# Loading K of pair 30 ahead of V of pair 29, with the usual split of pair 31's scores and a 24 KB + 8 KB last V

## The chip, the cores and the metric

The kernel runs on one core of one Trainium2 chip. The metric is device time in microseconds (us), the median of several executions. A profiled execution shows a span that is about 1.3 us shorter than its time (662.3 for a time of 663.57).

## The reference, cut to what matters

```python
B, D, Hq, Sk, Dh, F = 2, 512, 32, 8192, 128, 1376           # one query row per batch
q = layernorm(x) @ wq                                        # [B, 32 heads, 128]
scores = einsum("bhqd,bhkd->bhqk", q, k_cache) * Dh ** -0.5  # 64 (batch, head), 8192 keys each
o = einsum("bhqk,bhkd->bhqd", softmax(scores), v_cache)
h = x + o @ wo
h2 = h + ffn(layernorm(h))                                   # gate (ReLU), up, down
```

K and V together are 268 MB; each byte is used once. Everything else is small.

## The kernel before: the parts that matter

The kernel goes through 32 *pairs* (two heads of one batch). A K or a V of a pair is one 4 MB load into one of four slots: slot 0 K of even pairs, slot 1 V of even pairs, slots 2 and 3 the same for odd pairs. All loads go through one queue in program order. `J = 128` blocks of keys make up a pair.

The scores of a pair are split. VectorE does 96 of the 128 blocks (one multiply of K by q, four adds that halve the width, one reduce). TensorE does the other 32 in `NG = 4` groups of 8 (transpose on TensorE, evacuation by ScalarE, product with q). ScalarE takes the exp of both parts, and TensorE multiplies by V ("PV"), 32 matmuls a pair. After two pairs TensorE collects their outputs and VectorE normalizes and spreads them.

Pairs 0 to 29 run in loops on each engine; pairs 30 and 31 are written out as a tail, with the output product (O x Wo, then Wp) and the FFN behind them. Pair 31 gets a split of its own, eight TensorE groups and 64 blocks for VectorE:

```python
def split(p):
    n = 2 * NG if p == NP - 1 else NG
    return n, J - n * GT
```

TensorE in the tail (cut):

```python
collect(tail, 1)                              # pairs 28 and 29
k_part(tail, P0, (2, 3, 4, 5), ((k2p, 1),))   # K30; waits for VectorE's release k2p
...                                           # o_gather, O x Wo (30 matmuls), Wp (8 matmuls)
k_part(tail, P1, (9, 10, 11, 12, 14, 15, 16, 17), ((k2p, 2),))  # K31: eight groups
pv(tail, P0, ...)
pv(tail, P1, ...)                             # z_sum between its two parts
```

VectorE in the tail. It first needs TensorE's collect, and it is VectorE that tells TensorE (`k2p`) that a K is in:

```python
if p >= P0:
    if p == P0:
        dve.wait(t_ob_loop)                   # collect of pairs 28 and 29
        normalize(Ob, dve.run, dve.last)
        o_spread(g - 1, dve, dve.run(o_scale()))
    nc.vector.wait_ge(g2d, p - P0 + 1)
    nc.vector.wait_ge(slot_sem[s], 16)        # K of pair p has landed
    nc.vector.sem_inc(k2p, 1)                 # releases TensorE's k_part
    dve.last()
    t_dm[p] = dve.run(k_mult(p))
    k_adds(p, dve.run, dve.last)
    t_s[p] = dve.run(k_reduce(p))
```

The end of the load order is K29, V29, K30, K31, V30, V31 (two rows of 16 KB a partition), W_up, W_gate, W_down. The weights go into slot 0, so after K30 has been read.

The softmax here doesn't subtract the row's maximum and nothing guards it: scores larger than these inputs give would overflow.

Of the kernel before, what the change touches and what calls it, by code (L numbers as in the profile page):

```python
# [9 lines left out]
ALU = mybir.AluOpType  # L10
# [29 lines left out]
def bass_sequential_preLN__gqa_block_cached__glu_gated_reglu__decode_kernel(  # L40
# [24 lines left out]
    FR = F - 10 * 128  # L65
    VJ = 4
    PG = 2
    DR = (H - 2) * Dh // 128
# [6 lines left out]
    with ExitStack() as es:  # L75
# [87 lines left out]
        if True:  # L163

            def program():
# [145 lines left out]

                def split(p):
                    n = 2 * NG if p == NP - 1 else NG
                    return n, J - n * GT

                EV = 13
# [12 lines left out]
                def k_part(T, p, ev, k_wait):  # L329
                    s, ng = (2 * p) % 4, split(p)[0]  # L330
                    k_t = tile(s)
# [3 lines left out]
                    def score(g):  # L335
                        wait(a2p, ev[g])
                        kv_ = kT[g % 2][:].rearrange("p (k n r) -> p k r n", n=128, r=2)
                        for k in range(GT // 2):
                            jj = g * GT + 2 * k
                            for r in range(2):  # L340
                                i = nc.tensor.matmul(  # L341
                                    Sp[p % 2][:, 2 * jj:2 * jj + 4], lhsT=kv_[:, k, r, :],
                                    rhs=q_c[p % 2][:, 4 * r:4 * r + 4], start=(r == 0), stop=(r == 1))
                                if loop and g == ng - 2 and k == r == 0:
                                    T.mark(("kf", p), i)
                        if not loop:
                            T.mark(("sc", p, g), i)
                        elif g == ng - 1:
                            i.then_inc(p2a, 1)

                    for w in k_wait:
                        wait(*w)
                    for g in range(ng):
                        if g >= 2:
                            wait(a2p, ev[g - 2])
                        for k in range(GT // 2):
                            j = split(p)[1] + g * GT + 2 * k
                            i = nc.tensor.transpose(  # L358
                                Tp[g % 2][:, k * 128:(k + 1) * 128],
                                k_t[:, j:j + 2, :].rearrange("p j d -> p (j d)").bitcast(F32), ident_f[:])  # L360
# [4 lines left out]
                        if g >= 1:  # L365
                            score(g - 1)
                    score(ng - 1)

# [44 lines left out]
                with nc.Fori(0, NI, engines=OrderedEngineSet([nc.tensor.engine])):  # L413
                    jd = split(0)[1]
                    k_part(body, 0, (1, 2, 3, 4), ((k2p, 1),))
                    collect(body, 6)
                    pv(body, 0, ((jd, J, ((slot_sem[1], 16), (a2p, 5))), (0, jd, ((a2p, 7),))))
                    k_part(body, 1, (8, 9, 10, 11), ((k2p, 2),))
                    nc.tensor.wait_ge(l2p, 1)
                    o_gather(body)  # L420
                    nc.tensor.sem_inc(l2p, -1)
                    pv(body, 1, ((jd, J, ((slot_sem[3], 16), (a2p, 12))), (0, jd, ((a2p, EV),))))
                    z_sum(Ob)
# [8 lines left out]
                P0, P1 = NP - 2, NP - 1  # L432
                j30, j31 = split(P0)[1], split(P1)[1]
                collect(tail, 1)
# [10 lines left out]
                tail.mark("op", i)  # L445
                nc.tensor.wait_ge(a2p, 8)
                for c in range(DC):
                    nc.tensor.matmul(  # L448
                        Wp[:, c * B:(c + 1) * B], lhsT=os_sb[:].rearrange("p (n c) -> p c n", c=DC)[:, c, :], rhs=sel2[:],
                        start=False, stop=False, skip_group_check=True)  # L450
                k_part(tail, P1, (9, 10, 11, 12, 14, 15, 16, 17), ((k2p, 2),))
                pv(tail, P0, ((j30, J, ((slot_sem[1], 16), (a2p, 6))), (0, j30, ((a2p, 13),))))
                pv(tail, P1, ((j31, J, ((sem_vl[0], 16), (a2p, 18))), (0, j31, ((a2p, 19), (sem_vl[1], 16)))),
                   lambda: tail.mark("z", z_sum(Sp[0])))
# [14 lines left out]
                def exp(p, k, src):  # L469
                    q, jd_ = p % PG, split(p)[1]  # L470
                    j0, j1 = ((jd_, J), (0, jd_))[k]
                    for a in range(2):
# [45 lines left out]
                def k_mult(p):  # L518
                    jd_ = split(p)[1]
                    return nc.vector.tensor_tensor(  # L520
                        out=prod[:, 0:jd_, :], in0=tile((2 * p) % 4)[:, 0:jd_, :],
                        in1=q_c[p % 2][:, 8:QW].unsqueeze(1).broadcast_to([128, jd_, Dh]), op=ALU.mult)

                def k_adds(p, run, last):
                    jd_, w = split(p)[1], Dh
                    while w > 8:
                        w //= 2
                        last()
                        run(nc.vector.tensor_tensor(  # L529
                            out=prod[:, 0:jd_, 0:w], in0=prod[:, 0:jd_, 0:w], in1=prod[:, 0:jd_, w:2 * w], op=ALU.add))  # L530
                    last()

                def k_reduce(p):
                    jd_ = split(p)[1]
                    return nc.vector.tensor_reduce(  # L535
                        out=scores[p % PG][:, 0:jd_], in_=prod[:, 0:jd_, 0:8], axis=AX.X, op=ALU.add)

                def exp_pe(p):
                    n_ = split(p)[0] * GT
                    exp(p, 0, lambda h, a: Sp[p % 2][h, 0:2 * n_].rearrange(  # L540
                        "p (g j a) -> p g j a", a=2, j=VJ)[:, :, :, a])

                def exp_dve(p):
                    exp(p, 1, lambda h, a: scores[p % PG][h, 0:split(p)[1]].rearrange("p (g j) -> p g j", j=VJ))

# [62 lines left out]
                for p in range(NP):  # L608
                    s = (2 * p) % 4
                    ng, jd = split(p)  # L610
                    g = p // 2

                    if p >= P0:
                        if p == P0:
                            dve.wait(t_ob_loop)
                            normalize(Ob, dve.run, dve.last)
                            o_spread(g - 1, dve, dve.run(o_scale()))
                        nc.vector.wait_ge(g2d, p - P0 + 1)
# [3 lines left out]
                        t_dm[p] = dve.run(k_mult(p))  # L622
                        k_adds(p, dve.run, dve.last)
                        t_s[p] = dve.run(k_reduce(p))

                    if p < P1:
# [6 lines left out]

                    def evacs(g0=0, g1=ng):
                        for gg in range(g0, g1):
                            act.wait(tokp("pt", p, gg))
                            if gg >= 2:
                                act.wait(tokp("sc", p, gg - 2))
                            elif p == P1:
                                act.wait(tokp("sc", p - 1, NG - 2 + gg))  # L640
                            evac(gg)

                    if p == P0:
                        act.wait(tokp("pv", p - 1))
                        sums()
                        evacs()
                        act.wait(tokp("sc", p, ng - 1))
                        exp_pe(p)
                        act.wait(tok("og", NI))
                        to_pe(nc.scalar.activation(  # L650
                            out=O_all[:].rearrange("p r b -> p b r"),
                            in_=Op[1][:, 0:B * DR].rearrange("p (b r) -> p b r", r=DR), func=ACT.Copy))
                        act.wait(tok("op", NI))
                        to_pe(nc.scalar.activation(out=os_sb[:], in_=Op[1][:], func=ACT.Copy))
                    elif p == P1:
                        evacs(0, NG)
                        act.wait(t_s[P0])
                        exp_dve(P0)
                        evacs(NG)
                        act.wait(tokp("sc", p, ng - 1))  # L660
                        exp_pe(p)
                        act.wait(t_s[P1])
                        exp_dve(P1)

                    if p + 2 < NP:
                        sp.wait((d2s, p + 1), tokp("kf", p))
                        load(s, A_k_cache, p + 2)
                    if p < NP - 4:
                        sp.wait(tokp("pv", p))
                        load((2 * p + 1) % 4, A_v_cache, p + 2)  # L670
                    elif p == NP - 3:
                        sp.wait(tokp("pv", NP - 4))
                        load(1, A_v_cache, NP - 2)
                        sp.wait(tokp("pv", NP - 3))
                        for k, (j0, j1) in enumerate(((J // 2, J), (0, J // 2))):
                            nc.sync.dma_start(
                                slot[3][:, j0 * Dh:j1 * Dh],
                                kv(A_v_cache, NP - 1)[:, j0 * Dh:j1 * Dh]).then_inc(sem_vl[k], 16)
                    elif p == NP - 2:
                        sp.wait(t_dm[p], tokp("pt", p, NG - 1))  # L680
# [14 lines left out]
                sums()  # L695
                collect(tail, 20)
                dve.wait(tok("ob", NI))
# [140 lines left out]
```

## Time and profile before

| | kernel before |
|---|---|
| time, median of 3 | 662.72 us (662.57 to 663.37) |
| moved | 281.19 MB at a mean of 425 GB/s |
| PV of the last pair ends | 651.33 |
| TensorE's first FFN product starts | 654.62 |
| VectorE's last instruction starts | 660.00 |

The page of the kernel before, part 4, follows the chain of waits back from the end. Its line by engine:

```profile
DMA 76%; DVE 16%; PE 5%; ACT 2%; issue 1%; SPq 0%; DVEq 0%; ACTq 0%
...
```

Three quarters of that chain is loads that follow on one another, and the page's DMA row is at 90% or more in 39 of its 40 slices. So what a change can win without moving fewer bytes is to be looked for in the tail. The tail's VectorE, from the timeline of the kernel before (start in us, duration in us, engine, line, operation, out<-in, count, and in brackets what ended an idle time):

```profile
611.84 0.95 DVE L535 TENSOR_REDUCE scores<-prod 128x96 f32<-128x768 bf16 x1
619.03 0.17 DVE L482 TENSOR_REDUCE zr<-Ob 128x4 f32<-128x8 f32 x1 [6.25 <-PE Ob L394]
...
620.14 6.55 DVE L520 TENSOR_TENSOR prod<-slot,q_c 128x12288 bf16<-128x12288 bf16 x1
626.73 6.74 DVE L529 TENSOR_TENSOR prod<-prod 128x6144 bf16<-128x6144 bf16 x4
633.50 0.95 DVE L535 TENSOR_REDUCE scores<-prod 128x96 f32<-128x768 bf16 x1
634.49 4.42 DVE L520 TENSOR_TENSOR prod<-slot,q_c 128x8192 bf16<-128x8192 bf16 x1
...
643.72 0.69 DVE L535 TENSOR_REDUCE scores<-prod 128x64 f32<-128x512 bf16 x1
```

VectorE stands idle for 6.25 us after pair 29 (612.8 to 619.0), because it waits for TensorE's collect before it may touch K30. From there it works without a pause to 644.4.

The same stretch on TensorE, from the timeline of the kernel before:

```profile
613.69 2.74 PE L382 MATMUL O<-slot,e 128*16 128x512 bf16 x24 [4.67 <-ACT e L474]
...
617.13 1.87 PE L394 MATMUL Ob<-sel,os_sb 128*128 128x4 f32 x8 [0.17 <-ACT os_sb L550]
619.95 1.97 PE L358 MATMUL T<-ident_f,slot 128*128 128x128 f32 x8 [0.95 <-DVEq L620]
...
631.61 2.03 PE L448 MATMUL W<-sel,os_sb 128*128 128x2 f32 x8 [0.69 <-ACT os_sb L654]
633.62 1.97 PE L358 MATMUL T<-ident_f,slot 128*128 128x128 f32 x8
...
645.16 4.88 PE L382 MATMUL O<-slot,e 128*16 128x512 bf16 x48
...
650.29 1.04 PE L382 MATMUL O<-slot,e 128*16 128x512 bf16 x16
```

L382 is PV, L394 collect, L358 the transposes of a K, L448 Wp.

Stretches of time of the kernel before (start:end, length; busy time of PE, PEld, DVE, ACT, POOL with counts; granted TensorE clock, which is the share of its full speed that TensorE was allowed; DMA share; GB/s). The clock records hold only 0.50 ("half clock") and 1.00 ("full clock"); other values are means over a stretch.

```profile
620.00:625.00 5.00, 4.74 (x40) 3.82 (x40) 5.00 (x5) 3.27 (x4) 0.00 (x0) 0.50 1.04 446
635.00:640.00 5.00, 4.74 (x49) 3.70 (x48) 4.97 (x2) 4.34 (x8) 0.00 (x0) 0.50 1.01 429
645.00:650.00 5.00, 5.00 (x57) 1.75 (x55) 0.00 (x0) 1.57 (x8) 0.00 (x0) 0.55 1.00 420
650.00:655.00 5.00, 3.45 (x54) 2.44 (x51) 1.18 (x8) 0.60 (x1) 0.00 (x0) 1.00 0.92 369
655.00:656.00 1.00, 1.00 (x38) 1.00 (x35) 0.33 (x2) 0.00 (x0) 0.00 (x0) 1.00 0.30 115
656.00:657.00 1.00, 1.00 (x40) 0.92 (x38) 0.47 (x2) 0.00 (x0) 0.00 (x0) 0.65 0.02 6
```

The stream runs dry in the microsecond after 655, while the FFN is still running at 660.

### The profile page before, as it was taken

The numbers are of one execution on the slowest core, as the hardware profiler recorded it, in microseconds if no ns is written. First come the engines' busy times: TensorE is split into PE (matmuls) and PEld (weight loads), VectorE is DVE, ScalarE is ACT, GpSimd is POOL, SyncE is SP. The second block draws the span as 40 slices with busy tenths as digits, with TensorE's granted clock in tenths as the row PEclk, the third lists the DMA queues.
The fourth block names the chain that finished last, engine by engine and source line by source line (L and its number), as shares of the span: only waits on it lengthen the run. The fifth ranks groups of instructions, "written<-read, shape, count | busy, mean of one in ns | idle before, by whom it ended". The sixth has DMA issues, their size and how long they took to land.

```text
span 662.3 us, 7890 instructions
## 1 busy us (share of the span) xinstructions
PE 331.6 (50%) x3221; PEld 200.0 (30%) x3221; DVE 467.6 (71%) x285; ACT 215.9 (33%) x432; POOL 71.9 (11%) x121
## 2 busy tenths in 40 slices
PE   2652344445455453555645453554436455343787
PEld 2431322224232122333323232331214233121464
DVE  1775576788767678776767877676887767688691
ACT  0631332243343223334223333422334332232351
POOL 2002002020200202020020202002020200202000
PEclk9995565555756556755555567555675555557557
DMA  9999999999999999999999999999999999999995
GB/s 380 427 416 432 433 435 427 435 428 431 436 429 433 431 428 435 433 429 435 426 433 435 428 435 431 429 433 433 426 440 424 435 431 429 433 433 426 440 414 231
DMA packets 10782, 281.19 MB, mean 425 GB/s; under 512 B 1202, under 2 KB 1556, under 8 KB 1940
## 3 DMA queue, kind: packets, MB, share of 16 engines
q1 hardware_dynamic: 10760, 281.06, 98.9%
q8 instruction: 6, 0.10, 0.1%
q14 instruction: 4, 0.03, 0.0%
q10 hardware_dynamic: 12, 0.00, 0.0%
HBM read 281.05 MB, written 0.00 MB: 424 GB/s over the span
## 4 chain that ended last, share of the span: by engine, by line
DMA 76%; DVE 16%; PE 5%; ACT 2%; issue 1%; SPq 0%; DVEq 0%; ACTq 0%
DMA slot<-in_A_k_cache_dram 76%; DVE prod L520 15%; PE O L382 1%; PE T L358 1%; DVE prod L529 1%; ACT kT L547 1%; PE O L442 1%; PE Ob L394 0%; PE S L341 0%; PE W L448 0%; ACT e L474 0%; PE O L739 0%; PE S L739 0%; PE O L791 0%; ACT os_sb L550 0%
## 5 line engine op out<-in xcount | busy, mean ns | idle before, releaser
L520 DVE TENSOR_TENSOR prod<-slot,q_c 128x12288 bf16<-128x12288 bf16 (+1 forms) x32 | 207.7, 6492 | 144.9 <-DMA slot<-in_A_k_cache_dram 142.9
L382 PE MATMUL O<-slot,e 128*16 128x512 bf16 x1024 | 119.0, 619 | 214.7 <-ACT e L474 151.1
L529 DVE TENSOR_TENSOR prod<-prod 128x6144 bf16<-128x6144 bf16 (+4 forms) x128 | 210.3, 1643 | 7.8
L547 ACT ACTIVATE kT<-T 128x1024 bf16<-128x1024 bf16 x132 | 130.3, 1022 | 149.6 <-PE T L358 146.6
L358 PE MATMUL T<-ident_f,slot 128*128 128x128 f32 x528 | 117.6, 379 | 30.2 <-DVEq L568 29.1
L382 PEld LDWEIGHTS O<-slot,e 128*16 128x16 bf16 x1024 | 26.1, 113 | 281.8 <-ACT e L474 178.7
L358 PEld LDWEIGHTS T<-ident_f,slot 128*128 128x128 f32 x528 | 84.7, 194 | 45.6 <-DVEq L568 44.5
L474 ACT ACTIVATE e<-scores 64x96 bf16<-64x96 f32 (+1 forms) x64 | 19.4, 303 | 239.2 <-DVEq L582 238.8
L516 POOL COPY q_c<-q_all 128x136 bf16<-128x136 bf16 x32 | 57.1, 1788 | 198.2 <-DVEq L572 168.0
L341 PE MATMUL S<-q_c,kT 128*128 128x4 bf16 x1056 | 49.2, 169 | 39.2 <-ACT kT L547 38.5
L341 PEld LDWEIGHTS S<-q_c,kT 128*128 128x128 bf16 x1056 | 41.1, 105 | 68.0 <-ACT kT L547 66.6
L394 PE MATMUL Ob<-sel,os_sb 128*128 128x4 f32 x136 | 31.0, 351 | 24.0 <-ACT os_sb L550 24.0
L394 PEld LDWEIGHTS Ob<-sel,os_sb 128*128 128x128 f32 x136 | 29.5, 321 | 25.9 <-ACT os_sb L550 25.9
L499 POOL MEMSET O_l<- 128x40 bf16 (+1 forms) x13 | 1.8, 135 | 303.9 <-DVEq L579 303.9
L535 DVE TENSOR_REDUCE scores<-prod 128x96 f32<-128x768 bf16 (+1 forms) x32 | 30.2, 945 | 2.8
L547 ACT ACT_TABLE_LOAD x15 | 19.2, 1283 | 0.3
L474 ACT ACTIVATE e<-S 64x32 bf16<-64x32 f32 (+1 forms) x64 | 13.0, 203 | 15.2 <-PE S L341 14.8
L474 ACT ACTIVATION_READ_ACCUMULATOR e<-S 64x1 f32 x64 | 12.8, 201 | 0.7
L550 ACT ACTIVATE os_sb<-O 128x512 f32<-128x512 f32 x17 | 10.1, 597 | 7.7 <-PE O L382 7.3
L474 ACT ACTIVATION_READ_ACCUMULATOR e<-scores 64x1 f32 x64 | 11.8, 184 | 0.0
L403 PEld LDWEIGHTS Ob<-zs,ones_f 128*128 128x128 f32 x30 | 7.3, 303 | 12.7 <-issue 12.7
L299 ACT ACTIVATE q_all<-O 128x512 bf16<-128x512 f32 x8 | 4.4, 596 | 17.9 <-PE O L294 17.9
(94 smaller groups left out, 90.9 us busy)
## 6 DMA issues: line engine op xcount, KB each, us to landing
slot<-in_A_k_cache_dram SPq DMA_DIRECT2D x32, 4096.0 KB, 32.1
slot<-in_A_v_cache_dram SPq DMA_DIRECT2D x31, 4096.0 KB, 30.3
slot<-in_A_wq_dram SPq DMA_DIRECT2D x1, 4096.0 KB, 12.4
slot<-in_A_v_cache_dram SPq DMA_DIRECT2D x2, 2048.0 KB, 27.8
X<-in_A_wo_dram SPq DMA_DIRECT2D x1, 3840.0 KB, 46.7
slot<-in_B_W_up_dram SPq DMA_DIRECT2D x1, 1376.0 KB, 23.5
slot<-in_B_W_gate_dram SPq DMA_DIRECT2D x1, 1376.0 KB, 26.4
slot<-in_B_W_down_dram SPq DMA_DIRECT2D x2, 512.0 KB, 27.6
```

The source lines that it names most:

```text
L341: i = nc.tensor.matmul(Sp[p % 2][:, 2 * jj:2 * jj + 4], lhsT=kv_[:, k, r, :], rhs=q_c[p % 2][:, 4 * r:4 * r + 4], start=(r == 0), stop=(r ...
L358: i = nc.tensor.transpose(Tp[g % 2][:, k * 128:(k + 1) * 128], k_t[:, j:j + 2, :].rearrange("p j d -> p (j d)").bitcast(F32), ident_f[:])
L382: i = nc.tensor.matmul(Op[0][c:c + 16, :], lhsT=e_t[q][:, j // VJ, :], rhs=v_t[:, j:j + VJ, :].rearrange("p j d -> p (j d)"), start=(q == ...
L394: i = nc.tensor.matmul(Ob[:, 0:4], lhsT=os_sb[:, jj * Dh:(jj + 1) * Dh], rhs=sel[:, 4 * jj:4 * jj + 4], start=(jj == 0), stop=(jj == VJ - 1))
L403: return nc.tensor.matmul(bank[:, ZC:ZC + 8], lhsT=ones_f[:], rhs=zs[:], start=True, stop=True)
L474: i = nc.scalar.activation(out=e_t[q][h, j0 // VJ:j1 // VJ, 8 * q:8 * q + 8].rearrange("p g (j a) -> p g j a", a=2)[:, :, :, a], in_=src(h ...
L516: nc.gpsimd.tensor_copy(out=q_c[p % 2][:], in_=q_all[:, p]).then_inc(g2d, 1)
L520: return nc.vector.tensor_tensor(out=prod[:, 0:jd_, :], in0=tile((2 * p) % 4)[:, 0:jd_, :], in1=q_c[p % 2][:, 8:QW].unsqueeze(1).broadcast ...
L529: run(nc.vector.tensor_tensor(out=prod[:, 0:jd_, 0:w], in0=prod[:, 0:jd_, 0:w], in1=prod[:, 0:jd_, w:2 * w], op=ALU.add))
L535: return nc.vector.tensor_reduce(out=scores[p % PG][:, 0:jd_], in_=prod[:, 0:jd_, 0:8], axis=AX.X, op=ALU.add)
L547: to_pe(nc.scalar.activation(out=kT[gg % 2][:], in_=Tp[gg % 2][:].bitcast(BF16), func=ACT.Copy))
L550: to_pe(nc.scalar.activation(out=os_sb[:], in_=Op[0][:], func=ACT.Copy))
```

## The change

Intent: K30 is loaded ahead of V29, so that it is there when VectorE has finished pair 29. VectorE then does K30 at once and the normalize and spread of pairs 28 and 29 behind it. That leaves it the time for the usual 96 blocks of pair 31, and TensorE's eight groups for pair 31 become four. The last V comes as rows of 24 KB and 8 KB, so that only 8 PV matmuls hang on the last piece.

```diff
+    V_LAST = 32
...
-                def split(p):
-                    n = 2 * NG if p == NP - 1 else NG
-                    return n, J - n * GT
...
-                k_part(tail, P1, (9, 10, 11, 12, 14, 15, 16, 17), ((k2p, 2),))
-                pv(tail, P0, ((j30, J, ((slot_sem[1], 16), (a2p, 6))), (0, j30, ((a2p, 13),))))
-                pv(tail, P1, ((j31, J, ((sem_vl[0], 16), (a2p, 18))), (0, j31, ((a2p, 19), (sem_vl[1], 16)))),
+                k_part(tail, P1, (10, 11, 12, 13), ((k2p, 2),))
+                pv(tail, P0, ((JC, J, ((slot_sem[1], 16), (a2p, 6))), (0, JC, ((a2p, 8),))))
+                pv(tail, P1, ((V_LAST, J, ((sem_vl[0], 16), (a2p, 15))), (0, V_LAST, ((a2p, 15), (sem_vl[1], 16)))),
...
                     if p >= P0:
-                        if p == P0:
-                            dve.wait(t_ob_loop)
-                            normalize(Ob, dve.run, dve.last)
-                            o_spread(g - 1, dve, dve.run(o_scale()))
                         nc.vector.wait_ge(g2d, p - P0 + 1)
...
                         k_adds(p, dve.run, dve.last)
+                        if p == P0:
+                            dve.wait(tokp("pv", p - 2))
                         t_s[p] = dve.run(k_reduce(p))
+                        if p == P0:
+                            dve.wait(t_ob_loop)
+                            normalize(Ob, dve.run, dve.last)
+                            o_spread(g - 1, dve, dve.run(o_scale()))
...
-                    if p < NP - 4:
-                        sp.wait(tokp("pv", p))
-                        load((2 * p + 1) % 4, A_v_cache, p + 2)
-                    elif p == NP - 3:
...
-                        for k, (j0, j1) in enumerate(((J // 2, J), (0, J // 2))):
+                    v_loads = [p] if p < NP - 5 else [NP - 5] if p == NP - 4 else [NP - 4, NP - 3] if p == NP - 3 else []
+                    for r in v_loads:
+                        sp.wait(tokp("pv", r))
+                        if r < NP - 3:
+                            load((2 * r + 1) % 4, A_v_cache, r + 2)
+                    if p == NP - 3:
+                        for k, (j0, j1) in enumerate(((V_LAST, J), (0, V_LAST))):
```

(ScalarE does pair 30's second exp right after pair 30's own work and no longer in the middle of pair 31's; `split(p)` becomes a constant everywhere.)

More of the change, by code (lines that the diff above doesn't have):

```diff
@@ L329, in k_part @@
                 def k_part(T, p, ev, k_wait):
-                    s, ng = (2 * p) % 4, split(p)[0]
+                    s = (2 * p) % 4
                     k_t = tile(s)
@@ L343, in score @@
                                     rhs=q_c[p % 2][:, 4 * r:4 * r + 4], start=(r == 0), stop=(r == 1))
-                                if loop and g == ng - 2 and k == r == 0:
+                                if loop and g == NG - 2 and k == r == 0:
                                     T.mark(("kf", p), i)
@@ L347, in score @@
                             T.mark(("sc", p, g), i)
-                        elif g == ng - 1:
+                        elif g == NG - 1:
                             i.then_inc(p2a, 1)
@@ L352, in k_part @@
                         wait(*w)
-                    for g in range(ng):
+                    for g in range(NG):
                         if g >= 2:
@@ L356, in k_part @@
                         for k in range(GT // 2):
-                            j = split(p)[1] + g * GT + 2 * k
+                            j = JC + g * GT + 2 * k
                             i = nc.tensor.transpose(
@@ L366, in k_part @@
                             score(g - 1)
-                    score(ng - 1)
+                    score(NG - 1)
                 def pv(T, p, parts, between=None):
@@ L413, in program @@
                 with nc.Fori(0, NI, engines=OrderedEngineSet([nc.tensor.engine])):
-                    jd = split(0)[1]
                     k_part(body, 0, (1, 2, 3, 4), ((k2p, 1),))
                     collect(body, 6)
-                    pv(body, 0, ((jd, J, ((slot_sem[1], 16), (a2p, 5))), (0, jd, ((a2p, 7),))))
+                    pv(body, 0, ((JC, J, ((slot_sem[1], 16), (a2p, 5))), (0, JC, ((a2p, 7),))))
                     k_part(body, 1, (8, 9, 10, 11), ((k2p, 2),))
@@ L421, in program @@
                     nc.tensor.sem_inc(l2p, -1)
-                    pv(body, 1, ((jd, J, ((slot_sem[3], 16), (a2p, 12))), (0, jd, ((a2p, EV),))))
+                    pv(body, 1, ((JC, J, ((slot_sem[3], 16), (a2p, 12))), (0, JC, ((a2p, EV),))))
                     z_sum(Ob)
@@ L432, in program @@
                 P0, P1 = NP - 2, NP - 1
-                j30, j31 = split(P0)[1], split(P1)[1]
                 collect(tail, 1)
@@ L445, in program @@
                 tail.mark("op", i)
-                nc.tensor.wait_ge(a2p, 8)
+                nc.tensor.wait_ge(a2p, 9)
                 for c in range(DC):
@@ L469, in exp @@
                 def exp(p, k, src):
-                    q, jd_ = p % PG, split(p)[1]
-                    j0, j1 = ((jd_, J), (0, jd_))[k]
+                    q = p % PG
+                    j0, j1 = ((JC, J), (0, JC))[k]
                     for a in range(2):
@@ L518, in k_mult @@
                 def k_mult(p):
-                    jd_ = split(p)[1]
                     return nc.vector.tensor_tensor(
-                        out=prod[:, 0:jd_, :], in0=tile((2 * p) % 4)[:, 0:jd_, :],
-                        in1=q_c[p % 2][:, 8:QW].unsqueeze(1).broadcast_to([128, jd_, Dh]), op=ALU.mult)
+                        out=prod[:, 0:JC, :], in0=tile((2 * p) % 4)[:, 0:JC, :],
+                        in1=q_c[p % 2][:, 8:QW].unsqueeze(1).broadcast_to([128, JC, Dh]), op=ALU.mult)
                 def k_adds(p, run, last):
-                    jd_, w = split(p)[1], Dh
+                    w = Dh
                     while w > 8:
@@ L529, in k_adds @@
                         run(nc.vector.tensor_tensor(
-                            out=prod[:, 0:jd_, 0:w], in0=prod[:, 0:jd_, 0:w], in1=prod[:, 0:jd_, w:2 * w], op=ALU.add))
+                            out=prod[:, 0:JC, 0:w], in0=prod[:, 0:JC, 0:w], in1=prod[:, 0:JC, w:2 * w], op=ALU.add))
                     last()
                 def k_reduce(p):
-                    jd_ = split(p)[1]
                     return nc.vector.tensor_reduce(
-                        out=scores[p % PG][:, 0:jd_], in_=prod[:, 0:jd_, 0:8], axis=AX.X, op=ALU.add)
+                        out=scores[p % PG][:, 0:JC], in_=prod[:, 0:JC, 0:8], axis=AX.X, op=ALU.add)
                 def exp_pe(p):
-                    n_ = split(p)[0] * GT
+                    n_ = NG * GT
                     exp(p, 0, lambda h, a: Sp[p % 2][h, 0:2 * n_].rearrange(
@@ L543, in exp_dve @@
                 def exp_dve(p):
-                    exp(p, 1, lambda h, a: scores[p % PG][h, 0:split(p)[1]].rearrange("p (g j) -> p g j", j=VJ))
+                    exp(p, 1, lambda h, a: scores[p % PG][h, 0:JC].rearrange("p (g j) -> p g j", j=VJ))
                 def evac(gg):
@@ L609, in program @@
                     s = (2 * p) % 4
-                    ng, jd = split(p)
                     g = p // 2
                     if p >= P0:
-                        if p == P0:
-                            dve.wait(t_ob_loop)
-                            normalize(Ob, dve.run, dve.last)
-                            o_spread(g - 1, dve, dve.run(o_scale()))
                         nc.vector.wait_ge(g2d, p - P0 + 1)
@@ L632, in program, with evacs @@
                             q_copy(p + 1)
-                    def evacs(g0=0, g1=ng):
-                        for gg in range(g0, g1):
+                    def evacs():
+                        for gg in range(NG):
                             act.wait(tokp("pt", p, gg))
@@ L641, in evacs @@
                             evac(gg)
+                        act.wait(tokp("sc", p, NG - 1))
+                        exp_pe(p)
                     if p == P0:
@@ L646, in program @@
                         evacs()
-                        act.wait(tokp("sc", p, ng - 1))
-                        exp_pe(p)
                         act.wait(tok("og", NI))
@@ L652, in program @@
                             in_=Op[1][:, 0:B * DR].rearrange("p (b r) -> p b r", r=DR), func=ACT.Copy))
+                        act.wait(t_s[p])
+                        exp_dve(p)
                         act.wait(tok("op", NI))
@@ L655, in program @@
                     elif p == P1:
-                        evacs(0, NG)
-                        act.wait(t_s[P0])
-                        exp_dve(P0)
-                        evacs(NG)
-                        act.wait(tokp("sc", p, ng - 1))
-                        exp_pe(p)
-                        act.wait(t_s[P1])
-                        exp_dve(P1)
+                        evacs()
+                        act.wait(t_s[p])
+                        exp_dve(p)
                     if p + 2 < NP:
@@ L667, in program @@
                         load(s, A_k_cache, p + 2)
-                    if p < NP - 4:
-                        sp.wait(tokp("pv", p))
-                        load((2 * p + 1) % 4, A_v_cache, p + 2)
-                    elif p == NP - 3:
-                        sp.wait(tokp("pv", NP - 4))
-                        load(1, A_v_cache, NP - 2)
-                        sp.wait(tokp("pv", NP - 3))
-                        for k, (j0, j1) in enumerate(((J // 2, J), (0, J // 2))):
+                    v_loads = [p] if p < NP - 5 else [NP - 5] if p == NP - 4 else [NP - 4, NP - 3] if p == NP - 3 else []
[5 more added lines that the diff above has]
+                        for k, (j0, j1) in enumerate(((V_LAST, J), (0, V_LAST))):
                             nc.sync.dma_start(
@@ L678, in program @@
                                 kv(A_v_cache, NP - 1)[:, j0 * Dh:j1 * Dh]).then_inc(sem_vl[k], 16)
-                    elif p == NP - 2:
+                    if p == NP - 2:
                         sp.wait(t_dm[p], tokp("pt", p, NG - 1))
@@ L695, in program @@
                 sums()
-                collect(tail, 20)
+                collect(tail, 16)
                 dve.wait(tok("ob", NI))
```

## The prediction

> **What bounds it now.** The page gives 281.19 MB at a mean of 425 GB/s, DMA busy in tenths at 9 in 39 of 40 slices, and the chain of waits is 76% DMA. [...] One 4 MB load takes about 9.7 us. The change moves no byte, so nearly all of the 662.7 us stays. What can move is the tail after the stream. By windows of time the DMA share is 1.00 at 652-654 us, 0.66, 0.30 and 0.02 in the next microseconds: the last bytes arrive near 656.5. The kernel ends at 662.3. Behind the attention TensorE is the chain: pair 29's PV ends 616.4, collect to 619.0, K of 30 from 619.95, its scores to 626.1, O x Wo 627.35-630.9, Wp 631.6-633.6, K of 31 in eight groups 633.6-645.1, PV of 30 and 31 645.16-651.33, then 11 us of output and FFN.
>
> **What changes.** Stream today (landings): K29 598.2, V29 607.9, K30 617.7, K31 627.4, V30 637.1, V31 646.9, FFN weights up to 656.5. After: K29 598.2, K30 607.9, V29 617.7, the rest in place. The issues still come in time: K30 is issued at 585.6 (K28's multiply done), V29 right behind, K31 at 605, V30 at 605.4, V31 once pair 29's PV is done (about 621, while the queue has work to 637), weights near 629 (queue to 647). So I expect no DMA gap.
>
> - VectorE: K30's multiply starts at 612.9 (pair 29's reduce) instead of 620.1; with 6.56+6.74+0.95 us it ends at 627.2, then normalize and spread (1.1), K31's full multiply 628.4-642.7. VectorE ends a microsecond earlier than before (644.4) though it multiplies 96 columns of pair 31 instead of 64.
> - TensorE: V29 lands 9.7 later, so pair 29's PV ends near 621.0 (32 matmuls in 3.3 us after 617.7) instead of 616.4: +4.6. Collect is followed directly by K30 (today 0.95 us of wait for normalize): K30 from 623.5, i.e. +3.6. Pair 31 has four groups instead of eight: 6.2 us instead of 11.5, -5.3. PV of 30 begins at 643.4 instead of 645.16: -1.7.
> - PV of 30 and 31 is the same 64 matmuls (0.10 us each at granted clock 0.50, about 0.06 at 1.00). exp of pair 31 is out by 645.2, before PV of 30 is done. V31's 3 MB land near 644.4, its last 1 MB at 646.9: no wait. End of PV near 649.7; [...]
>
> **On the path.** About 1.6 us of tail. A floor is set by the weights: the last W_down block lands at 656.5 and the FFN's last product ends at 659.9, so no more than about 2.8 us can be won without waiting for the weights.
>
> **Prediction.** 661.2 us, 80% range 660.2 to 662.6. Faster by over 2%: 0.01; within 2%: 0.98; slower by over 2%: 0.01.
>
> **Signs.** Right: DMA still full to 655-656; K30 multiply near 612.9; PE waits for V29 until about 617.7; PV of pair 31 ends 648.5-650; FFN waits on no weight, or only briefly. Wrong steps would show as: a DMA gap near 605, 621 or 629; VectorE's score of 31 later than 643.5; PE waiting for V31's last piece; FFN groups waiting for DMA.
>
> **What would make it wrong.** V31's issue waiting past 637 (then each us of gap is a us lost); slower DMA with the 24 KB and 8 KB rows; TensorE at half clock in all of PV and FFN, which would eat the 1.6 us; or weights landing later.

The sum: 4.6 us later with V29, 3.6 at the start of K30, 5.3 us less for the four groups, so PV begins 1.7 us earlier and ends near 649.7 instead of 651.33. That is about 1.6 us, and 662.7 less that is about the 661.2. The remarks under "What would make it wrong" on a gap, on 24 KB and 8 KB rows and on half clock are estimates; only the rows were put to a test (runs 11 and 12). What single steps took at each clock can be read in the kernel before: collect 1.87 us at 0.50 (from 617.13) and 1.05 at 1.00 (from 652.03), 24 PV products 2.74 us at 0.50 (from 613.69), 16 of them 1.04 at 1.00 (from 650.29).

## More of the kernel before

K31 starts at 633.62, exactly when Wp ends (631.61 + 2.03 = 633.64) and also just when VectorE issues pair 30's reduce (633.50) and with it K31's release.

TensorE is 95% busy in 620 to 625 and 635 to 640 and still has the half clock, 0.50. These two stretches are mostly transposes.

## The result, and the profile after

| | before | after |
|---|---|---|
| time, median of 4 | 662.64 us (661.88 to 663.37) | 661.01 us (660.88 to 661.48) |
| same, in a later session | 662.76 (11 runs, 662.07 to 664.1) | 661.05 (5 runs, 660.78 to 661.85) |
| span of the profiled run | 662.3 | 659.7 |
| PV of the last pair ends | 651.33 | 647.65 |
| first FFN product starts | 654.62 | 650.94 |
| VectorE's last instruction starts | 660.00 | 657.47 |

The ratio is 0.9977 with an interval of 0.996 to 0.9994, and 0.9975 (0.9963 to 0.9988) in the later session. The gain of about 1.6 us is small and clear of noise. The two profiled runs differ by 2.6 us, more than the medians do, because the profiled run of the kernel before (663.57) was one of its slower ones.

The chain of waits of the kernel after, from its page:

```profile
DMA 80%; DVE 18%; issue 1%; PE 1%; SPq 0%; DVEq 0%
...
```

TensorE is down from 5% to 1%. The end of that chain in order of time shows why (start, duration, what):

```profile
627.07 26.18 DMA slot<-in_B_W_gate_dram
653.25 0.04 issue
653.30 1.73 PE O L730 x44
...
```

The chain no longer goes back through TensorE's work on pairs 30 and 31: it ends in the landing of the gate weights, 653.25, and the FFN's gate products right behind it. VectorE of the kernel after:

```profile
613.55 6.56 DVE L514 TENSOR_TENSOR prod<-slot,q_c 128x12288 bf16<-128x12288 bf16 x1 [1.04 <-DVEq L577]
620.14 6.73 DVE L523 TENSOR_TENSOR prod<-prod 128x6144 bf16<-128x6144 bf16 x4
626.91 0.95 DVE L528 TENSOR_REDUCE scores<-prod 128x96 f32<-128x768 bf16 x1
...
628.88 6.55 DVE L514 TENSOR_TENSOR prod<-slot,q_c 128x12288 bf16<-128x12288 bf16 x1
...
642.24 0.95 DVE L528 TENSOR_REDUCE scores<-prod 128x96 f32<-128x768 bf16 x1
```

K30's multiply starts at 613.55 instead of 620.14, and pair 31's scores are out at 643.19 instead of 644.41, though VectorE now does half as many blocks again for pair 31. TensorE of the kernel after:

```profile
617.42 3.59 PE L379 MATMUL O<-slot,e 128*16 128x512 bf16 x32 [14.26 <-DMA slot<-in_A_v_cache_dram]
...
621.71 1.05 PE L391 MATMUL Ob<-sel,os_sb 128*128 128x4 f32 x8 [0.17 <-ACT os_sb L543]
622.63 1.07 PE L355 MATMUL T<-ident_f,slot 128*128 128x128 f32 x8
...
629.02 0.29 PE L405 MATMUL O<-rsel,O_l 128*128 128x30 bf16 x4 [0.91 <-DVE O_l L500]
...
635.80 1.95 PE L355 MATMUL T<-ident_f,slot 128*128 128x128 f32 x8
...
641.92 4.88 PE L379 MATMUL O<-slot,e 128*16 128x512 bf16 x56
...
647.04 0.61 PE L379 MATMUL O<-slot,e 128*16 128x512 bf16 x8
...
653.30 1.71 PE L730 MATMUL O<-d_b,slot 128*128 128x2 bf16 x44 [0.31 <-DMA slot<-in_B_W_gate_dram]
```

TensorE starts the tail later, as V29 now lands at 617.4 instead of 607.9: it is idle for 14.26 us, and pair 29's PV ends at 621.01 instead of 616.43. It is earlier again by 641.92 (PV of 30 and 31; 645.16 before), because pair 31 has four groups. The waits for the normalize's spread (0.91 us at 629.02) and for the gate weights (0.31 us at 653.30) are new. Stretches of the kernel after:

```profile
620.00:625.00 5.00, 4.15 (x41) 2.97 (x34) 4.93 (x3) 2.30 (x3) 0.00 (x0) 0.84 1.05 452
635.00:640.00 5.00, 4.74 (x36) 4.28 (x36) 4.93 (x3) 2.56 (x3) 0.00 (x0) 0.50 0.98 419
645.00:650.00 5.00, 3.96 (x58) 2.17 (x50) 0.51 (x3) 0.60 (x1) 0.00 (x0) 0.96 1.01 426
650.00:655.00 5.00, 4.17 (x122) 3.79 (x119) 1.46 (x8) 0.00 (x0) 0.00 (x0) 0.72 0.92 369
655.00:656.00 1.00, 0.69 (x33) 0.62 (x36) 0.41 (x3) 0.00 (x0) 0.00 (x0) 0.50 0.23 88
656.00:657.00 1.00, 0.72 (x29) 0.44 (x20) 0.00 (x0) 0.00 (x0) 0.00 (x0) 0.50 0.00 0
```

The stream ends where it ended before: the DMA shares of the last three stretches are the same within 0.07. The granted clock is not the same: 0.84 instead of 0.50 in 620 to 625, 0.96 instead of 0.55 in 645 to 650, and 0.72 instead of 1.00 in 650 to 655. By the clock records the last full-clock stretch lasts 6.83 us in both kernels and runs from 645.4 to 652.2 instead of 649.5 to 656.3. It begins 3.5 us into PV instead of 4.3, and ends 1.3 us after the FFN's first product instead of 1.7.

So, in the profiled runs: PV of the last pair ends 3.68 us earlier (651.33 to 647.65). From there to the first FFN product both take 3.29 us. The FFN, from its first product to VectorE's last instruction, takes 6.53 us (650.94 to 657.47) instead of 5.38 (654.62 to 660.00), which gives 1.15 us back. Of that, 0.62 us lie ahead of the gate products (650.94 to 653.30 against 654.62 to 656.36; 0.31 of it is the wait for the weights, the rest slower products), and 0.53 us between the start of W_down's products and the end (655.46 to 657.47 against 658.52 to 660.00; 0.28 of it is a pause among the products, until 656.74, for which the profile names no releaser; W_down's last block had landed by 656.4). Together -3.68 + 1.15 = -2.53 us.

### The profile page after: what moved, and what is told of

Its sections match the earlier page's. It is cut to its first block, busy times and chain, and to the rows that moved or that the text cites. A ratio compares the mean times of both kernels' runs of the same rounds, so it can differ in the third digit from the quotient of the medians.

```text
span 659.7 us, 7791 instructions
## 1 busy us (share of the span) xinstructions
PE 323.9 (49%) x3173; PEld 194.0 (29%) x3173; DVE 471.7 (71%) x285; ACT 211.9 (32%) x428; POOL 72.1 (11%) x121
## 4 chain that ended last, share of the span: by engine, by line
DMA 80%; DVE 18%; issue 1%; PE 1%; SPq 0%; DVEq 0%
DMA slot<-in_A_k_cache_dram 76%; DVE prod L514 16%; DMA slot<-in_B_W_gate_dram 4%; DVE prod L523 2%; PE O L730 0%; PE O L782 0%; DVE scores L528 0%; SPq L169 0%; SPq L175 0%; DVEq L561 0%; SPq L178 0%; DVEq L565 0%; SPq L172 0%; DVE kT L789 0%; DVE hd L763 0%
## 5 line engine op out<-in xcount | busy, mean ns | idle before, releaser
L514 DVE TENSOR_TENSOR prod<-slot,q_c 128x12288 bf16<-128x12288 bf16 x32 | 209.9, 6558 | 145.8 <-DMA slot<-in_A_k_cache_dram 142.7
L523 DVE TENSOR_TENSOR prod<-prod 128x6144 bf16<-128x6144 bf16 (+3 forms) x128 | 212.3, 1658 | 7.8
L540 ACT ACTIVATE kT<-T 128x1024 bf16<-128x1024 bf16 x128 | 126.2, 1022 | 145.9 <-PE T L355 143.3
L355 PE MATMUL T<-ident_f,slot 128*128 128x128 f32 x512 | 111.5, 373 | 29.1 <-DVEq L561 29.0
L469 ACT ACTIVATE e<-scores 64x96 bf16<-64x96 f32 x64 | 19.4, 304 | 239.7 <-DVEq L575 238.9
L355 PEld LDWEIGHTS T<-ident_f,slot 128*128 128x128 f32 x512 | 80.9, 191 | 44.3 <-DVEq L561 44.3
L338 PE MATMUL S<-q_c,kT 128*128 128x4 bf16 x1024 | 47.5, 168 | 39.6 <-ACT kT L540 38.9
L338 PEld LDWEIGHTS S<-q_c,kT 128*128 128x128 bf16 x1024 | 39.4, 104 | 67.1 <-ACT kT L540 65.9
L528 DVE TENSOR_REDUCE scores<-prod 128x96 f32<-128x768 bf16 x32 | 30.5, 953 | 2.8
L469 ACT ACTIVATE e<-S 64x32 bf16<-64x32 f32 x64 | 13.0, 202 | 15.1 <-PE S L338 14.7
```

The source lines that it names most:

```text
L338: i = nc.tensor.matmul(Sp[p % 2][:, 2 * jj:2 * jj + 4], lhsT=kv_[:, k, r, :], rhs=q_c[p % 2][:, 4 * r:4 * r + 4], start=(r == 0), stop=(r ...
L355: i = nc.tensor.transpose(Tp[g % 2][:, k * 128:(k + 1) * 128], k_t[:, j:j + 2, :].rearrange("p j d -> p (j d)").bitcast(F32), ident_f[:])
L469: i = nc.scalar.activation(out=e_t[q][h, j0 // VJ:j1 // VJ, 8 * q:8 * q + 8].rearrange("p g (j a) -> p g j a", a=2)[:, :, :, a], in_=src(h ...
L514: return nc.vector.tensor_tensor(out=prod[:, 0:JC, :], in0=tile((2 * p) % 4)[:, 0:JC, :], in1=q_c[p % 2][:, 8:QW].unsqueeze(1).broadcast_t ...
L523: run(nc.vector.tensor_tensor(out=prod[:, 0:JC, 0:w], in0=prod[:, 0:JC, 0:w], in1=prod[:, 0:JC, w:2 * w], op=ALU.add))
L528: return nc.vector.tensor_reduce(out=scores[p % PG][:, 0:JC], in_=prod[:, 0:JC, 0:8], axis=AX.X, op=ALU.add)
```

## The experiments

Theory at the start: the tail is a chain on TensorE; the later V29 costs it 4.6 us, four groups less in pair 31 win more than that, and the early K30 is what lets VectorE take over the blocks. The rivals: one of the parts alone is the gain, or the bytes are.

**1. The usual split without the new order** (on the kernel before).

```diff
-                    n = 2 * NG if p == NP - 1 else NG
+                    n = NG
-                k_part(tail, P1, (9, 10, 11, 12, 14, 15, 16, 17), ((k2p, 2),))
+                k_part(tail, P1, (9, 10, 11, 12), ((k2p, 2),))
```
(and the counts of the waits behind it)

> Old stream order, VectorE in its old order, but pair 31 with the usual 96 columns on VectorE and four TensorE groups. Theory (the split is only affordable with K30 early, because VectorE is the last engine without it): VectorE starts K31's multiply at 634.5 as before and needs 6.56+6.74+0.95 us, so its scores are out at 648.8 instead of 644.4, exp at 649.6; 24 PV matmuls follow in about 2.6 us; the PV ends near 652.3 instead of 651.3, time 663 to 664.6, so slower than before by about 1 us. Rival (fewer TensorE groups are the whole gain, the order of the loads is decoration): 661.0 like the kernel after.

Measured: 665.31 us (664.98 to 666.48), before 662.76; ratio 1.0039 (1.0026 to 1.0052). Slower, as the theory says, but by 2.5 us where it expected about 1 (663 to 664.6). Lines of its timeline:

```profile
647.74 0.95 DVE L535 TENSOR_REDUCE scores<-prod 128x96 f32<-128x768 bf16 x1
...
649.54 0.59 PE L403 MATMUL S<-zs,ones_f 128*128 128x8 f32 x2 [5.93 <-ACT e L474]
```

VectorE's scores are out at 648.69 (theory: 648.8), and TensorE waits 5.93 us for the exp behind them. PV ends at 652.81 (expected 652.3). VectorE alone is the tail here. The rival, that fewer groups are the whole gain, falls.

**2. The new order with eight groups** (on the kernel after: pair 31 gets its old `split` back, and V31 its two halves; VectorE keeps its new order).

```diff
-                k_part(tail, P1, (10, 11, 12, 13), ((k2p, 2),))
+                k_part(tail, P1, (10, 11, 12, 13, 14, 15, 16, 17), ((k2p, 2),))
-    V_LAST = 32
+    V_LAST = 64
```
(and `split(p)` put back wherever the kernel before had it)

> New stream order and new order on VectorE, but pair 31 keeps its 64 columns on VectorE and eight TensorE groups, V31 in two halves. Theory (V29 landing 9.7 us later makes TensorE later, and four fewer groups pay for it): TensorE starts K31 near 635.8 as in the kernel after, the eight groups take about 11 us instead of 6.1, the PV ends near 652.5 to 653, time 665 to 666.5, slower than before by 3 to 4 us. Rival (the early K30 and the idle VectorE time it fills are the gain by themselves): at or below 661.

Measured: 664.83 us (663.27 to 667.42); ratio 1.0039 (1.0019 to 1.006). Slower by about 2 to 2.6 us, a little less than expected (3 to 4), with a wide spread; the profiled run (664.21) is one of the faster ones. Lines of its timeline:

```profile
636.79 1.95 PE L359 MATMUL T<-ident_f,slot 128*128 128x128 f32 x8
...
647.78 2.77 PE L383 MATMUL O<-slot,e 128*16 128x512 bf16 x48
```

K31 takes TensorE from 636.79 to 647.8, eleven microseconds, and PV starts 5.9 us later than in the kernel after. The rival falls: the new order by itself loses. In the profiled run the clock had already risen when PV began: 48 matmuls took 2.77 us, where the kernel after needed 4.88 for 56. That is the likely reason why it ended less late than expected. The rise came at about 646.3 (granted clock 0.50 in 640 to 645, 0.87 in 645 to 650), when TensorE had done nothing but K31's transposes and scores since Wp ended at 636.9.

**3. The kernel after, with the normalize ahead of K30 on VectorE.**

```diff
                     if p >= P0:
+                        if p == P0:
+                            dve.wait(t_ob_loop)
+                            normalize(Ob, dve.run, dve.last)
+                            o_spread(g - 1, dve, dve.run(o_scale()))
                         nc.vector.wait_ge(g2d, p - P0 + 1)
...
                         k_adds(p, dve.run, dve.last)
-                        if p == P0:
-                            dve.wait(tokp("pv", p - 2))
                         t_s[p] = dve.run(k_reduce(p))
-                        if p == P0:
-                            dve.wait(t_ob_loop)
-                            normalize(Ob, dve.run, dve.last)
-                            o_spread(g - 1, dve, dve.run(o_scale()))
```

> The kernel after, but VectorE waits for pair 29's PV and does the normalize and spread before K30's work, as the kernel before did. Theory (the early K30 is worth nothing unless VectorE is free to take it): K30's multiply starts near 623.9 instead of 613.6, K31's scores are out about 9 to 10 us later (near 652), time 668 to 671. Rival (TensorE alone is the chain of the tail): within 1 us of the kernel after.

Measured: 671.7 us (668.3 to 672.55); ratio 1.0126 (1.0106 to 1.0146). More than ten microseconds behind the kernel after in the median, a little beyond what was expected. The runs fall into two groups, two at 668.3 and 668.5 and four from 671.4 to 672.6; the profiled one (668.5) is of the first, so what the slower group lost besides is not shown. In its timeline ScalarE's copy ahead of Wp, which stands behind pair 30's exp, makes TensorE wait, and the exp of pair 31 makes it wait once more:

```profile
639.61 2.03 PE L443 MATMUL W<-sel,os_sb 128*128 128x2 f32 x8 [5.39 <-ACT os_sb L649]
...
653.42 1.47 PE L379 MATMUL O<-slot,e 128*16 128x512 bf16 x24 [2.23 <-ACT e L469]
```

VectorE took up K30 at 623.83, as expected. So moving K30 in the stream is a loss without moving the normalize behind it, at least with ScalarE's new order, which this run keeps: the 5.39 us of wait come from pair 30's exp standing ahead of the copy, and the early K30 with ScalarE's old order was not run.

**4. The kernel after again**, in the session of 1 to 3.

> The kernel after unchanged, for comparison on the same chip: 660.9 to 661.5, 1.2 to 2 us under the kernel before; its trace should again show V31's last piece landing about 1 us before its last PV, and the FFN within 0.5 us of the landing of the gate weights.

Measured: 661.05 us (660.78 to 661.85); ratio 0.9975 (0.9963 to 0.9988). As expected: V31's last piece landed at 646.9 and the last 8 PV matmuls ended at 647.65; the gate weights landed at 653.5 and their products started at 653.54.

Together the four make a table of medians:

| | old order | new order |
|---|---|---|
| eight groups in pair 31 | 662.76 | 664.83 |
| four groups in pair 31 | 665.31 | 661.05 |

"New order" means the loads, VectorE's normalize and ScalarE's exp of pair 30 together; the exp was never moved by itself, and splits between four and eight groups were not run. Either part alone loses 2 to 2.6 us; the two together win 1.7.

**5 and 6. Only a sliver of the FFN weights** (wrong results), in the kernel before and in the kernel after. Each weight load is cut to 256 elements a partition, some 9 us of stream; slot and waits stay.

```diff
-                                slot[0][:, k * DC * F:(k + 1) * DC * F],
-                                w.rearrange("(p c) n -> p (c n)", c=DC)).then_inc(sem_w[k], 16)
+                                slot[0][:, k * DC * F:k * DC * F + 256],
+                                w.rearrange("(p c) n -> p (c n)", c=DC)[:, 0:256]).then_inc(sem_w[k], 16)
```
(W_down's three loads likewise)

> The kernel before with only a sliver of each FFN weight block loaded (wrong result on purpose; about 3.9 MB, 9 us of stream, less; all waits kept). Theory (before, the end is set by TensorE's chain behind the last scores, and no weight is waited for): 662.7 as the kernel before, within 0.4. Rival (the kernel is bound by its bytes to the end): shorter by the 9 us that the stream is shorter, 654.

> The same cut in the kernel after (wrong result on purpose). Theory (the tail has come within half a microsecond of the landing of the gate weights): the wait of 0.3 to 0.5 us ahead of the gate products goes, and the time falls by 0.3 to 0.8 against the kernel after, to about 660.5. Rival (bytes alone): 9 us less, 652. Other rival (weights are not waited for even now): no change, 661.0.

Measured: before with slivers 663.29 us, the unchanged kernel before 663.19 in that session, ratio 1.0007 (0.9994 to 1.0021): no change, as expected. After with slivers 661.35 us (660.37 to 661.7), ratio to the kernel before 0.9976 (0.9962 to 0.9989), the same as the whole kernel after had in its own session (0.9975). The 0.3 to 0.8 us that were expected did not show in the times. In the profiled run, the fastest of the five (660.37), the wait for the gate weights is gone:

```profile
652.99 1.72 PE L730 MATMUL O<-d_b,slot 128*128 128x2 bf16 x44
```

The products start at 652.99 instead of 653.30, the pause among W_down's products is gone too (run 4, with all its weights, has no such pause either), and the time is 0.59 us under the profiled run of the kernel after (660.96). So the weights cost the kernel after somewhere between nothing and 0.6 us, which these runs do not settle. That bytes bind to the very end falls: 9 us of stream less bought less than a microsecond in either kernel.

The profiled run of the kernel before with slivers is of use for another reason. Its time is 661.63, the lowest of its five and 1.7 us below their median. One of its stretches:

```profile
616.00:619.00 3.00, 1.67 (x16) 1.49 (x13) 0.96 (x9) 0.60 (x1) 0.00 (x0) 1.00 0.99 426
```

Here the granted clock is 1.00 during pair 29's collect, which took 1.06 us; in the profiled run of the kernel before it is 0.50 there and the collect took 1.87. K30's multiply started at 618.96 instead of 620.14, and PV ended 2.2 us earlier. No weight is waited for in either of these two runs, and their tails part at the collect. So, by this one pair, the moment at which the clock rises can move the time by about as much as the change does. That this is also the cause of the spread of the unprofiled runs is likely and not shown.

**7 and 8. Less TensorE work in the tail**, in the kernel before and in the kernel after: 4 instead of 30 O x Wo products (most of the attention output of pairs 0 to 29 is left out; the comparison with the reference passes even so, presumably because the attention output is small beside x, so says nothing about this part).

```diff
-                for r in range(DR):
+                for r in range(4):
                     i = nc.tensor.matmul(
                         Op[1][32 * (r % 4):32 * (r % 4) + B, :], lhsT=O_all[:, r, :], rhs=X[:, r * D:(r + 1) * D],
-                        start=(r < 4), stop=(r >= DR - 4))
+                        start=True, stop=True)
```

> The kernel before with 4 instead of 30 of the O x Wo products in the tail (wrong result on purpose): about 3.1 us of TensorE work less on the chain ahead of K31. Theory (TensorE's chain is the tail, with 2.8 us of room until the weights): V31's last piece at 646.9 and the weights stop it, so the time falls by 1.5 to 2.7 us, to 660.0 to 661.2, level with the kernel after. Rival (VectorE or the stream is the tail): no change, 662.7.

> The same cut of TensorE work in the kernel after (wrong result on purpose). Theory (the change has used up the room: pair 31's exp on VectorE's scores is out at 644.2, V31's pieces land at 644.4 and 646.9, the gate weights at 653.5): the cut buys at most 0.5 us, 660.5 to 661.4. Rival (TensorE's chain is still alone on the path): 3 us less, 658.

Measured, in the kernel before: 662.96 us (662.12 to 663.92) against 663.19, ratio 0.9996 (0.9983 to 1.001). Nothing, where the theory said 1.5 to 2.7 us. This is a clear miss, and its timeline says what was overlooked:

```profile
628.65 2.03 PE L448 MATMUL W<-sel,os_sb 128*128 128x2 f32 x8 [0.70 <-ACT os_sb L654]
633.63 1.97 PE L358 MATMUL T<-ident_f,slot 128*128 128x128 f32 x8 [2.95 <-DVEq L620]
```

Wp is 2.96 us earlier (628.65 instead of 631.61), and then TensorE waits 2.95 us for VectorE's queue at line 620, the release of K31. K31 starts at 633.63, as always. VectorE's release and the end of Wp had been within 0.14 us of each other in the kernel before (633.50 and 633.64), and the chain of its profile goes back from K31 to Wp alone.

In the kernel after: 660.69 us (660.5 to 661.28), ratio to the kernel before 0.9967 (0.9953 to 0.998); the whole kernel after had 0.9975. At most half a microsecond, as expected. The 3 us are lost in a wait for V31's first piece:

```profile
639.17 3.59 PE L379 MATMUL O<-slot,e 128*16 128x512 bf16 x32
644.28 2.74 PE L379 MATMUL O<-slot,e 128*16 128x512 bf16 x24 [1.51 <-DMA slot<-in_A_v_cache_dram]
```

and in the 24 matmuls behind the pause, which took 2.74 us (granted clock 0.50 in 640 to 645, 0.68 in 645 to 650).

**9 and 10. Two tied chains?** The new theory: in the kernel before, VectorE (normalize, K30, release of K31) and TensorE (K30, O x Wo, Wp) reach K31 together, so relieving one buys nothing. VectorE is relieved by giving the release right after pair 30's first add, when K31 has just landed (627.4):

```diff
+                        def release(r):
+                            nc.vector.wait_ge(g2d, r - P0 + 1)
+                            nc.vector.wait_ge(slot_sem[(2 * r) % 4], 16)
+                            nc.vector.sem_inc(k2p, 1)
...
-                        k_adds(p, dve.run, dve.last)
+                        k_adds(p, dve.run, dve.last, (lambda: release(P1)) if p == P0 else None)
```
(`k_adds` calls it behind its first add; pair 31's q is copied earlier for it; run 10 has the cut of run 7 too)

> The kernel before, but VectorE tells TensorE that K31 is in (it lands at 627.4) right after its first add of pair 30, not after pair 30's reduce at 633.6; nothing else moves. New theory, after the cut of TensorE work in the kernel before bought nothing because TensorE then waited 2.95 us for VectorE's release of K31: in the kernel before VectorE (pair 29's normalize, K30, release at 633.6) and TensorE (O x Wo, Wp until 633.6) are tied, so this alone buys nothing: 662.7 within 0.5. Rival (VectorE's late release alone is the cause): 1.5 us or more faster.

> The early release of K31 and the cut of 26 O x Wo products together, in the kernel before (its result leaves out most of A's output on purpose). New theory (two tied chains, each hides the other): K31 starts near 630.6, pair 31's exp on VectorE's scores at 645.2 and V31's last piece at 646.9 stop it, PV ends near 648.6; the time falls by 1.5 to 2.7 us to 660.2 to 661.4, though either part alone buys nothing. Rival (neither chain is the cause): no change.

Measured: early release alone 663.32 us (662.94 to 664.1), ratio 1.0009 (0.9995 to 1.0023): nothing. In its timeline the wait for the release is gone, and K31 starts at 633.25, when Wp ends. Both together 661.56 us (660.86 to 662.37), ratio 0.9982 (0.9967 to 0.9998): faster by about 1.2 us, though the interval nearly reaches 1. The median is a little above the expected 660.2 to 661.4. In the timeline of both together K31 starts with the end of Wp and PV ends at 648.19:

```profile
628.36 2.03 PE L448 MATMUL W<-sel,os_sb 128*128 128x2 f32 x8 [0.70 <-ACT os_sb L662]
630.25 1.95 PE L358 MATMUL T<-ident_f,slot 128*128 128x128 f32 x8
...
647.15 1.04 PE L382 MATMUL O<-slot,e 128*16 128x512 bf16 x16
```

Each part alone buys nothing and the two together do: in the kernel before the tail had two chains of the same length up to K31.

**11 and 12. The last V's rows**, 24 KB and 8 KB in the kernel before, 16 KB and 16 KB in the kernel after.

```diff
-                        for k, (j0, j1) in enumerate(((J // 2, J), (0, J // 2))):
+                        for k, (j0, j1) in enumerate(((32, J), (0, 32))):
```
```diff
-    V_LAST = 32
+    V_LAST = 64
```

> The kernel before with V31 in rows of 24 KB and 8 KB instead of two of 16 KB, nothing else. Theory (V31's pieces land at 642.0 and 646.9, PV of pair 31 asks for them at 648.5 and 650.3): no change, 662.7 within 0.5. Rival (the split of the last V is part of the gain by itself): faster by 0.5 or more.

> The kernel after with V31 in two rows of 16 KB. Theory: 40 instead of 56 matmuls can run before z and the last piece at 646.9, and 16 instead of 8 behind it, 0.4 to 0.5 us more of PV, partly hidden in the wait for the gate weights: 661.0 to 661.6. Rival (the 24 and 8 KB split carries the gain): back to 662.5.

Measured: 663.37 us (660.88 to 664.28) in the kernel before, which had 662.82 (661.65 to 664.12) in that session, ratio 1.0004 (0.9985 to 1.0024): no change. In the kernel after 661.25 us (660.94 to 661.48), ratio 0.9976 (0.9962 to 0.9989), the same as with 24 and 8 KB. Its trace shows a wait of 0.20 us for the last piece and PV's end at 647.86 instead of 647.65. The rows carry next to nothing of the gain.

No version that ran beats the kernel after as a correct kernel. Run 8 says that a shorter TensorE chain would be worth about half a microsecond at most as the loads stand, and run 6 that earlier weights would be worth no more than that.

## Why the prediction was right, and where it was not

The time, 661.2 predicted and 661.01 measured, was right, and so was its frame: the stream stays as it is, and what is won lies in the tail and comes up against the weights at the end. How near the number came is in part luck. In the profiled runs PV ended 2 us earlier than predicted (647.65 for 649.7); the FFN took back 1.15 us that the sum did not have, and the other 0.9 us are what the profiled run of the kernel before was slower than its median. Point by point, with the profiled run of the kernel after:

| step | predicted | measured |
|---|---|---|
| the stream has no gap | full to 655-656 | share 0.92 in 650-655, 0.23 in 655-656, as before |
| K30's multiply starts | 612.9 | 613.55 |
| PV of pair 29 ends | 621.0 | 621.01 |
| K30 starts on TensorE | 623.5 | 622.63 |
| pair 31's scores out on VectorE | 642.7 | 643.19 |
| PV of 30 and 31 starts | 643.4 | 641.92 |
| PV ends | 649.7 | 647.65 |
| FFN waits for weights | no, or briefly | 0.31 us |

- The sizes that were off belong to the granted clock. K31 starts on TensorE 2.2 us later than before (635.80 against 633.62) where the sum had 3.6; the four groups then win 5.4 us as predicted (6.12 against 11.54). Pair 29's PV is now 32 matmuls in one go (3.59 us) instead of 8 and 24 with a pause, and the clock rises right behind it: 0.84 in 620 to 625. Collect took 1.05 us instead of 1.87, and K30's first transposes 1.07 instead of 1.97. The same rise is in the traces of runs 3, 4, 6, 8 and 12 (0.91 to 1.00 in 621 to 624), and not in that of run 2 (0.50), where 32 PV matmuls took the same 3.59 us (from 617.24; 617.42 in the kernel after). In the kernel before, 24 PV matmuls that took 2.73 us (from 594.98) were followed by a granted clock of 0.95 in 598 to 601, and the same 24 in 2.74 us (from 613.69) by 0.50 in 616 to 619 and in 620 to 625. What decides whether the rise comes is not shown; no run here was made to find out.
- The clock took a little of it back. The FFN took 6.53 us instead of 5.38, but only some 0.3 us of the 1.15 can be the clock's: the products ahead of the gate products were that much slower, as full clock ended sooner (652.2, 1.3 us after the FFN's first product, instead of 1.7 us after it); the 44 products of W_up took 1.71 us instead of 1.56. Another 0.31 us is the wait for the gate weights. The gate products (1.71 us, before 1.73) and W_down's ran at half clock in both kernels (0.50 from 652.2 on, and before from 656.3 on); the 0.53 us that W_down's part took longer are the pause of 0.28 us and a rest, and neither is explained.
- The step that failed is in the reading of the kernel before: "Behind the attention TensorE is the chain". It was half of the truth. VectorE's chain through normalize and K30 to the release of K31 was tied with it. Run 7 took 3 us off TensorE's chain and won nothing; runs 9 and 10 showed that it takes both. The prediction came out right all the same: it summed up both engines step by step, and the change relieves both.
- That coupling is what the two by two table shows. The old order cannot afford the usual split, because VectorE starts K30 at 620.1, behind the normalize, and is out with pair 31 only at 648.7 (run 1). The new order cannot afford eight groups, because V29 comes 9.5 us later (617.4 instead of 607.9) and K31 starts later on TensorE (636.79 in run 2, 633.62 before).
- What bounds the kernel now is the stream and what must come behind it. V31's last piece lands at 646.6 and PV ends at 647.65; the gate weights land at 653.25 and their products start at 653.30. A cut of 3 us of TensorE work (run 8) or of 9 us of stream (run 6) wins about half a microsecond or nothing.

The mean over the whole span of the kernel after is 426 GB/s, and single slices read up to 443. Its first and its last slice (382 and 291 GB/s) are the lowest, and no run here tried to win any of that.

## What to carry to other kernels

When a tail is short of time on two engines, look for releases that come within a tenth or two of a microsecond of each other: here the profile named one, and relieving either one alone won nothing. Test it by cutting work out of the supposed chain, with a wrong result if need be, and see what the next instruction then waits for. And treat a new order of loads and the new split of work that it makes possible as one change: here each half alone was a loss of 2 to 2.6 us and the whole a gain of 1.7.
